# Attention, routed experts and a SwiGLU layer in one kernel: output weights combined on another engine, weight casts issued a block ahead, and activation splits issued earlier

## The chip, the cores and the metric

The kernel runs on one core of a Trainium2 chip. The metric is the device time of one execution in microseconds (us). Before the change three runs took 1058.4, 1061.27 and 1061.85 us, the median being 1061.27 us.

## The reference

Three layers follow one another. The first is attention with a sigmoid in place of the softmax: 4 batches, 12 heads, 448 tokens, heads of 64.

```
scores = (1 / sqrt(64)) * q @ k.T - log(448)
x = sigmoid(scores) @ v                      # 1792 tokens x 768
```

The second is a layer of 8 experts. Each token goes to the expert with the largest logit and is scaled by that expert's softmax probability.

```
e = argmax(x @ w_gate)                        # 768 -> 8
y = prob[e] * (relu(x @ w1[e]) @ w2[e])       # 768 -> 1024 -> 768
```

The third is a dense SwiGLU layer with 1536 hidden columns.

```
g = y @ w2_gate
out = (g * sigmoid(g) * (y @ w2_val)) @ w2_out
```

The weights of the third layer arrive as 64-bit floats. [...]

## The kernel before, in words

**Products in three parts.** TensorE multiplies numbers of a reduced float32 type. To keep the precision each float32 operand is split in a high half (a cast to the reduced type, on ScalarE) and a low half (operand minus high half, on VectorE), and a product is made of three matmuls: high by high, high by low, low by high. `split` (L75) issues the two instructions for one block one after the other.

**Stages.** Attention comes first, then the expert stage (`product` with `kind` 0 and 1, tiles `hps` and `yps`), then the SwiGLU stage (`strassen`, L849, tiles `pa` to `pd`), then the output stage (`product2`, L1406, tiles `oa` to `od`). The third layer's products use the Strassen-Winograd scheme: a 2x2 block product is made of seven products, numbered 1 to 7, of sums and differences of blocks. Their results are added up in PSUM and by VectorE.

**Order of the work.** All of it is written out by hand: each engine executes its instructions in the order in which the program issues them, and an instruction that waits holds up those behind it on its engine. In the expert stage, `when` ties an item of side work to a weight block; in the SwiGLU stage, `at_step` and `later` tie it to a step of the list `steps`. There are 24 rounds of seven products, two rounds to a pair, so 168 steps of nine matmuls each. Most pairs run the products of one round and then those of the other in the order 1, 6, 5, 7, 2, 3, 4. Three pairs (rounds 0 and 1, 10 and 11, 12 and 13) alternate the two rounds and end with 4, 3 instead. `advance` runs after the matmuls of a step are issued: first the evacuations due, then the side work of the step, then the preparation of weights.

**Weight blocks.** `prep` (L730) splits the block for a product five steps ahead of it (`AHEAD`). A block is either a part of a raw tile `w` or a sum `sr`. The sums are made by `sum_w` on GpSimd in the first twelve rounds, stored by SP to DRAM, and loaded again in the other twelve. A raw tile is loaded by SP once its buffer has been released, which the program counts in `left`. In the output stage `prep2` does the same for halves of the activation blocks, and makes their sums on VectorE (`sum_h`).

**Evacuation.** A pair keeps its two rounds side by side in PSUM tiles: `a` for the products 1 and 2, `c` for 5 and 3, `d` for 7 and 4. `c` and `d` are the two buffers of one pool. In `evac` (L884) the products 3 and 4 have `u` added in place in their PSUM tile. `finish_tile` (L869) then takes the value: for the even round, the one of the gate, ScalarE makes a sigmoid `m` and VectorE the product `m` = value times `m`; for the odd round, VectorE makes `h` = value times the even round's `m`, which is stored to DRAM.

**Activation splits.** At the start of the SwiGLU stage `split_all(0, n)` splits the activation block for product `n`: three casts and three subtractions. Block 6 is split ahead of the loop; blocks 5, 7, 4 and 3 at the steps of the products 6, 5, 7 and 4 of round 0.

**Output weights.** They are converted in the background, in six parts `j`: `load_o` loads two raw tiles into a "room", `convert_o` converts them, `combine_o` (L1168) makes four differences of 128x384 on GpSimd, `store_o` (L1176) stores the seven combinations to DRAM by SP. Three parts are done in the expert stage and three in the SwiGLU stage. Near the end of that stage `load_wo` and `split_wo` bring the weights for products 1 and 6; the other 15 pieces follow in the output stage.

Of the kernel before, what the change touches and what calls it, by code (L numbers as in the profile page):

```python
# [9 lines left out]
F32 = mybir.dt.float32  # L10
# [12 lines left out]
def sigmoid_attention_moe_swiglu_kernel(  # L23
# [683 lines left out]
    def a_block(r, i, k):  # L707
        left[r, i - 1] -= 1
        return wraws[r, i - 1][:, (k - 1) * HK:k * HK]
# [20 lines left out]
    def prep(r, n):  # L730
        m = {5: 1, 6: 2, 7: 3, 3: 4}.get(n)
        if m is None:
            s = a_block(r, *{1: (1, 1), 2: (1, 2), 4: (2, 2)}[n])
        else:
            s = sums[r, m]
        hi = early.tile([P, HK], F32R, tag="wgh", name="wgh", bufs=AHEAD + 1)
        lo = early.tile([P, HK], F32R, tag="wgl", name="wgl", bufs=AHEAD + 1)
        split(hi, lo, s)
        wst[r, n] = (hi, lo)
        if m is not None and r < R1:  # L740
            nc.sync.dma_start(wsd[r, m - 1], s)

    state = {"load": 0, "sum": 0, "prep": 0, "now": 0}

# [8 lines left out]
    def sum_to(m):  # L753
        load_more()
        while state["sum"] < min(m, len(steps)) and (steps[state["sum"]][0], 1) in wraws:
            sum_w(*steps[state["sum"]])
            state["sum"] += 1

    def prep_to(m):
        m = min(m, len(steps))  # L760
        while state["prep"] < m:
            sum_to(state["prep"] + 5)
            prep(*steps[state["prep"]])
            state["prep"] += 1
        sum_to(m + 4)

    rows = {}
# [85 lines left out]
    def bank(r, nm):  # L853
        return banks[r // 2, nm][:, r % 2, :TH]
# [29 lines left out]
    def evac(r, n):  # L884
        V = nc.vector
        k = place[r, n] + 1
        if n == 1:
            if (r, "p1") not in sb:
                t = sb[r, "p1"] = et("p", 2)
                nc.scalar.copy(t, bank(r, "a"))  # L890
        elif n == 6:
            t = sb[r, "u"] = et("u", 2)
            V.tensor_add(t, banks.pop((r, "b"))[:, :TH], sb.pop((r, "p1")))
        elif n == 5:
            t = sb[r, "p5"] = et("p", 2)
            nc.scalar.copy(t, bank(r, "c"))  # L896
        elif n == 7:
            t = et("c", 3)
            V.tensor_add(t, bank(r, "d"), sb.pop((r, "p5")))  # L899
            nc.gpsimd.tensor_tensor(t, sb[r, "u"], t, op=ALU.add)  # L900
            finish_tile(k + 2, r, 2, 2, t, nc.gpsimd)
        elif n == 2:
            finish_tile(k, r, 1, 1, bank(r, "a"), V)
        else:
            t = bank(r, {3: "c", 4: "d"}[n])
            V.tensor_add(t, t, sb[r, "u"])
            finish_tile(k + 1, r, *{3: (1, 2), 4: (2, 1)}[n], t, V)

    turn = [2]
# [114 lines left out]
    def when(kind, s, j, f):  # L1024
        at.setdefault((kind, s, j), []).append(f)
# [131 lines left out]
    JO = 3  # L1157
# [7 lines left out]
            room["parts"] = convert(room["ro", x], room["u"], room["w", x].bitcast(F32), True)  # L1165
        room["parts"][g]()

    def combine_o(j):  # L1168
        w0, w1, u = (room[k].bitcast(F32).rearrange("p (x d) -> p x d", x=2)
                     for k in (("w", 0), ("w", 1), "u"))  # L1170
        t4 = room["t4"].bitcast(F32)
        for o, x, y in ((u[:, 0], w0[:, 1], w0[:, 0]), (u[:, 1], w1[:, 1], u[:, 0]),
                        (w0[:, 1], w1[:, 1], w0[:, 1]), (t4, w1[:, 0], u[:, 1])):
            nc.gpsimd.tensor_tensor(o, x, y, op=ALU.subtract)

    def store_o(j):  # L1176
        for n, t in ((2, ("w", 1)), (0, ("w", 0)), (4, "u"), (6, "t4")):
# [70 lines left out]
    with tc.manual_schedule():  # L1248
# [92 lines left out]
        def h_block(q, i, k, h):  # L1341
            j = KD * (k - 1) + K3 * h
            return raw2[q % 2, i][:, j:j + K3].rearrange("p j t -> p (j t)")

        def sum_h(q, m, h):
            V = nc.vector
            if m == 1:
                V.tensor_add(ss[q % 2, 1, h], h_block(q, 2, 1, h), h_block(q, 2, 2, h))
            elif m == 2:
                V.tensor_sub(ss[q % 2, 2, h], ss[q % 2, 1, h], h_block(q, 1, 1, h))  # L1350
            elif m == 3:
                V.tensor_sub(h_block(q, 2, 1, h), h_block(q, 1, 1, h), h_block(q, 2, 1, h))
            else:
                V.tensor_sub(ss[q % 2, 2, h], h_block(q, 1, 2, h), ss[q % 2, 2, h])

        def prep2(q, n, h):
            s = {1: lambda: h_block(q, 1, 1, h), 2: lambda: h_block(q, 1, 2, h),
                 4: lambda: h_block(q, 2, 2, h), 5: lambda: ss[q % 2, 1, h],
                 6: lambda: ss[q % 2, 2, h], 7: lambda: h_block(q, 2, 1, h),
                 3: lambda: ss[q % 2, 2, h]}[n]()  # L1360
            hi = early.tile([P, HK], F32R, tag="wgh", name="hhi", bufs=AHEAD + 1)
            lo = early.tile([P, HK], F32R, tag="wgl", name="hlo", bufs=AHEAD + 1)
            split(hi, lo, s)
            hst[q, n, h] = (hi, lo)
            if h == 0:
                return
            x = 1 if (q, n) == (0, 6) else q if n == 1 and q != 1 else None
            for m in (4,) if n == 7 else (1, 2, 3) if x is not None else ():
                for y in range(2):
                    sum_h(q if n == 7 else x, m, y)  # L1370
            if n == 4 and q + 2 < NQ:
                for i in (1, 2):
                    load_h(q + 2, i)

# [1 line left out]

        def prep2_to(m):
            while state2["prep"] < min(m, len(halves)):
                prep2(*halves[state2["prep"]])
                state2["prep"] += 1  # L1380

        banks2 = {}
        sb2 = {}

# [82 lines left out]
        def at_step(r, n, f, d=0):  # L1467
            todo.setdefault(place[r, n] + d, []).append(f)

        def split_all(p, n, eng=None):  # L1470
            for j in range(K3):
                split_x(p, n, j, eng if j == 2 else None)

        for n in ORD2[2:]:
            if n != 2:
                at_step(0, {5: 6, 7: 5, 4: 7, 3: 4}[n], lambda n=n: split_all(0, n))
        for t in range(2):
            at_step(2 + 2 * t, 1, lambda t=t: load_rows(1, t))
            for j in range(KD):
# [22 lines left out]

        for j in range(JO, KD):
            if j <= JO + 1:
                key = ((1, 6), (R1, 1))[j - JO]
                at_step(*key, lambda j=j: next_room(j))
            b0 = ((2, 1), (R1 + 1, 5), (R1 + 1, 5))[j - JO]
            d = 20 * (j == KD - 1)
            for x in range(2):
                for g in range(4):  # L1510
                    at_step(*b0, lambda j=j, x=x, g=g: convert_o(j, x, g), d + 8 * x + 2 * g)
            at_step(*b0, lambda j=j: combine_o(j), d + 14)
            at_step(*b0, lambda j=j: store_o(j), d + 18)
            if j == JO + 1:
                at_step(*b0, lambda j=j: load_o(j + 1, 0), d + 6)
                at_step(*b0, lambda j=j: load_o(j + 1, 1), d + 14)
# [8 lines left out]
                raw2[0, i] = yt([P, K2, P], "hraw")  # L1525

        early_wo = [(n, i) for n in (1, 6) for i in range(3)]
        base = (NR - 6, ORD[3])
        at_step(*base, first_wo)
        for k, (n, i) in enumerate(early_wo):  # L1530
            at_step(*base, lambda n=n, i=i: load_wo(n, i), 1 + 3 * k)
            at_step(*base, lambda n=n, i=i: split_wo(n, i), 5 + 3 * k)
        for i in (1, 2):
            at_step(*base, lambda i=i: load_h(0, i), 16 + 3 * i)

        def second_raw():
            raw2[1, 1] = raw_tile(post, "z2")
            load_h(1, 1)

        at_step(*base, second_raw, 25)  # L1540

        def first_sums():
            t = hsp.tile([P, FF], F32, tag="hs", name="s2v", bufs=1)
# [107 lines left out]
```

## Time and profile before

| | before |
|---|---|
| runs, us | 1058.4, 1061.27, 1061.85 |
| the profiled execution, us | 1062.1 |
| its span, us | 1060.2 |
| mean granted TensorE clock | 0.991 |
| busy, us: TensorE, its weight loads | 1016.6, 820.2 |
| busy, us: VectorE, ScalarE, GpSimd | 787.4, 590.3, 354.7 |

The span goes from the first to the last instruction of the profiled execution. In the rows below PE is TensorE, PEld its weight loads, DVE VectorE, ACT ScalarE, POOL GpSimd, and SP the engine that issues most transfers; a q behind an engine's name means its sequencer. "L849" is a line of the kernel. Shapes are partitions x elements. Attention takes the first 203 us of the span, the expert stage runs to about 561, the SwiGLU stage to about 893, the output stage to the end.

### The profile page before, as it was taken

What the parts mean: (1) busy time and instruction counts of PE and PEld (TensorE: products, weight loads), DVE (VectorE), ACT (ScalarE), POOL (GpSimd) and SP (SyncE); (2) the same over time, 40 slices, a digit from 0 to 9 for tenths busy, and PEclk for the clock granted to TensorE, in tenths of its full rate; (3) what the DMA queues carried; (4) which work ended last, traced back from release to release, by engine and by line L of the source; (5) the groups of instructions that cost most, each with busy time, mean ns of one, the idle gap of its engine ahead of it and who ended that gap; (6) DMA issues with size and microseconds to landing.
All of it is one profiled execution on the core that took longest, in us unless ns stands there. A gap on an engine that the chain in (4) does not pass through costs nothing. (4 is left out here: it accounts for less than half of the span.)

```text
span 1060.2 us, 16991 instructions
## 1 busy us (share of the span) xinstructions
PE 1016.6 (96%) x5640; PEld 820.2 (77%) x5640; DVE 787.4 (74%) x1279; ACT 590.3 (56%) x941; POOL 354.7 (33%) x303
## 2 busy tenths in 40 slices
PE   8999999999999989999997899999999999999995
PEld 6566556567776767777786789998799899999995
DVE  3776878788877868776687887868988777966651
ACT  6666666446776767676675344455534443733331
POOL 2665566620133331411011665652234222010111
PEclk9999999999999999999999999999999999999998
DMA  8998988756878695688754557534665782653310
GB/s 192 278 269 241 288 245 238 290 179 226 310 249 304 243 345 190 211 324 292 249 180 163 164 160 227 177 120 153 228 220 164 238 247 91 241 167 119 104 46 30
DMA packets 162862, 222.83 MB, mean 210 GB/s; under 512 B 56096, under 2 KB 127008, under 8 KB 162768
## 3 DMA queue, kind: packets, MB, share of 16 engines
q1 hardware_dynamic: 153424, 188.99, 56.3%
q0 software_dynamic: 6864, 31.68, 8.3%
q10 hardware_dynamic: 2480, 1.02, 0.3%
q8 instruction: 46, 0.75, 0.3%
q14 instruction: 48, 0.39, 0.1%
HBM read 217.89 MB, written 55.66 MB: 258 GB/s over the span
## 5 line engine op out<-in xcount | busy, mean ns | idle before, releaser
L985 DVE TENSOR_TENSOR wlo<-wraw,whi 128x768 fp32r<-128x768 f32 (+1 forms) x186 | 204.3, 1123 | 71.0 <-ACT whi L983 66.5
L983 ACT CAST whi<-wraw 128x768 fp32r<-128x768 f32 (+1 forms) x186 | 170.1, 927 | 91.8 <-PE yps L1007 46.9
L242 ACT ACTIVATE a<-sc,logs 112x896 f32<-112x896 f32 x96 | 91.9, 1017 | 60.5 <-PE sc L240 60.4
L849 PE MATMUL pd<-x,wgh 128*128 128x448 f32 x288 | 85.3, 378 | 7.9 <-DVE h L877 4.8
L80 DVE TENSOR_TENSOR wgl<-sr,wgh 128x384 fp32r<-128x384 f32 x96 | 68.9, 722 | 25.9 <-ACT wgh L79 24.9
L849 PE MATMUL pc<-x,wgh 128*128 128x448 f32 x288 | 84.9, 375 | 3.2 <-DVE x L823 1.7
L900 POOL TENSOR_TENSOR c<-u,c 128x448 f32<-128x448 f32 x24 | 35.7, 1489 | 155.1 <-DVE c L899 141.1
L849 PE MATMUL pa<-x,wgh 128*128 128x448 f32 x288 | 82.8, 369 | 0.9 <-PEq L1296 0.9
L251 PE MATMUL pu<-a,vraw 112*64 112x448 f32 x384 | 77.5, 545 | 0.0
L174 POOL TENSOR_SCALAR w<-w 128x768 f32<-128x768 f32 x24 | 54.7, 2278 | 62.1 <-ACT w L162 62.0
L79 ACT CAST wgh<-sr 128x384 fp32r<-128x384 f32 x96 | 48.9, 513 | 35.3 <-PE pd L849 18.2
L849 PEld LDWEIGHTS pd<-x,wgh 128*128 128x128 f32 x288 | 54.5, 193 | 15.5 <-ACT p L896 5.5
L849 PEld LDWEIGHTS pc<-x,wgh 128*128 128x128 f32 x288 | 54.4, 191 | 10.0 <-DVE x L823 2.6
L1007 PE MATMUL yps<-wlo,hh 128*128 128x384 f32 x216 | 56.6, 343 | 3.7 <-DVE wlo L985 3.5
L1007 PE MATMUL yps<-whi,hh 128*128 128x384 f32 x216 | 58.7, 352 | 0.0
L849 PEld LDWEIGHTS pa<-x,wgh 128*128 128x128 f32 x288 | 53.7, 189 | 6.3 <-issue 1.3
L251 PEld LDWEIGHTS pu<-a,vraw 112*64 112x64 f32 x384 | 25.4, 136 | 40.9 <-issue 40.7
L1007 PE MATMUL yps<-whi,hl 128*128 128x384 f32 x216 | 55.5, 337 | 0.1
L80 DVE TENSOR_TENSOR wgl<-w,wgh 128x384 fp32r<-128x384 f32 x72 | 47.5, 661 | 9.4 <-ACT wgh L79 9.3
L849 PE MATMUL pc<-x,wgl 128*128 128x448 f32 x144 | 53.7, 373 | 0.6 <-DVE wgl L80 0.6
L1424 POOL DMA_INDIRECT out_dram<-ot,perm_c x12 | 12.5, 1044 | 124.2 <-DVE hlo L80 71.6
L849 PE MATMUL pd<-x,wgl 128*128 128x448 f32 x144 | 54.0, 375 | 0.0
(310 smaller groups left out, 2572.2 us busy)
## 6 DMA issues: line engine op xcount, KB each, us to landing
wraw<-in_moe_w_dram SPq DMA_DIRECT2D x108, 384.0 KB
wraw<-in_moe_w_dram SPq DMA_DIRECT2D x78, 512.0 KB
ring<-in_moe_w_dram SPq DMA_DIRECT2D x30, 512.0 KB
ring<-in_moe_w_dram SPq DMA_DIRECT2D x40, 384.0 KB
w<-wgd SPq DMA_DIRECT2D x36, 384.0 KB
hraw<-hd SPq DMA_DIRECT2D x13, 768.0 KB
r<-in_moe_w_gate_dram SPq DMA_DIRECT2D x12, 768.0 KB
wgd<-w POOLq DMA_DIRECT2D x24, 384.0 KB, 6.4
```

The source lines that it names most:

```text
L79: nc.scalar.copy(hi, src)
L80: nc.vector.tensor_sub(lo, src, hi.bitcast(F32))
L174: nc.gpsimd.tensor_scalar(w, w, TINY, None, op0=ALU.is_ge)
L242: nc.scalar.activation(am[i][:, c], sc[:CP, :, :S], AF.Sigmoid, bias=logs[:CP], scale=SCALE)
L251: nc.tensor.matmul(pu[h * D:(h + 1) * D, :S], vt[:, h, c], a[:, c, h], start=(c == 0), stop=(c == C - 1))
L849: nc.tensor.matmul(ps, st[:, a], mv[:, j], start=(j == 0 and m == 0 and n not in (2, 3, 4)), stop=(j == K3 - 1 and m == 2), skip_group_che ...
L900: nc.gpsimd.tensor_tensor(t, sb[r, "u"], t, op=ALU.add)
L983: nc.scalar.copy(hi[:, :w], r)
L985: nc.vector.tensor_sub(lo[:, :w0], r[:, :w0], hi[:, :w0].bitcast(F32))
L1007: nc.tensor.matmul(ps[:, m, :w], st[:, a], mv[:, m * w:(m + 1) * w], start=(j == 0 and i == 0), stop=(j == m_ - 1 and i == 2))
L1424: nc.gpsimd.indirect_dma_start(out=out[:, :], out_offset=bass.IndirectOffsetOnAxis(ap=perm_c[:, t:t + 1], axis=0), in_=ot.rearrange("p m d ...
```

## The change

The differences of the output weights move from GpSimd to VectorE, in two halves of two each, which are issued at different places; each half of the stores follows its half of the differences. `prep` issues the cast of a block and returns its subtraction, which is issued behind the next block's cast, with the store of the sum and the release of the raw tile; `prep2` likewise, and its sums are made ahead of a cast instead of behind a split. In `evac` the sum of the products 3 and 4 goes to an SBUF tile instead of staying in PSUM where the pair's last step has the same number. The activation splits of blocks 5, 7, 4 and 3 are issued earlier. The last two rooms and the early output weights get later steps, the latter closer together.

```diff
     def prep(r, n):
...
+            s = wraws[r, i - 1][:, (k - 1) * HK:k * HK]
...
-        split(hi, lo, s)
         wst[r, n] = (hi, lo)
-        if m is not None and r < R1:
-            nc.sync.dma_start(wsd[r, m - 1], s)
+        nc.scalar.copy(hi, s)
+
+        def low():
+            nc.vector.tensor_sub(lo, s, hi.bitcast(F32))
+            if m is None:
+                left[r, i - 1] -= 1
+            elif r < R1:
+                nc.sync.dma_start(wsd[r, m - 1], s)
+        return low
...
-            prep(*steps[state["prep"]])
+            lows.append(prep(*steps[state["prep"]]))
+            if len(lows) > 1:
+                lows.pop(0)()
             state["prep"] += 1
+        if m == len(steps) and lows:
+            lows.pop(0)()
...
-            t = bank(r, {3: "c", 4: "d"}[n])
-            V.tensor_add(t, t, sb[r, "u"])
+            ps = bank(r, {3: "c", 4: "d"}[n])
+            t = et("c", 3) if steps[min(k // 14 * 14 + 13, len(steps) - 1)][1] == n else ps
+            V.tensor_add(t, ps, sb[r, "u"])
...
-    def combine_o(j):
+    def combine_o(h):
...
-        for o, x, y in ((u[:, 0], w0[:, 1], w0[:, 0]), (u[:, 1], w1[:, 1], u[:, 0]),
-                        (w0[:, 1], w1[:, 1], w0[:, 1]), (t4, w1[:, 0], u[:, 1])):
-            nc.gpsimd.tensor_tensor(o, x, y, op=ALU.subtract)
+        for o, x, y in (((u[:, 0], w0[:, 1], w0[:, 0]), (u[:, 1], w1[:, 1], u[:, 0])),
+                        ((w0[:, 1], w1[:, 1], w0[:, 1]), (t4, w1[:, 0], u[:, 1])))[h]:
+            nc.vector.tensor_sub(o, x, y)
...
-        when(*seq[spots[c + 3]], lambda j=j: combine_o(j))
-        when(*seq[spots[c + 4]], lambda j=j: store_o(j))
+        for h in range(2):
+            when(*seq[spots[c + 3 + h] + 1 - h], lambda h=h: combine_o(h))
+            when(*seq[spots[c + 4] + 2 * h], lambda j=j, h=h: store_o(j, h))
...
         def prep2(q, n, h):
+            x = {(0, 6, 1): 1, (q, 1, 0): q}.get((q, n, h))
+            for m in (4,) if (n, h) == (7, 1) else () if x is None or (q, x) == (1, 1) else (1, 2, 3):
+                for y in range(2):
+                    sum_h(q if m == 4 else x, m, y)
...
-            split(hi, lo, s)
             hst[q, n, h] = (hi, lo)
...
+            nc.scalar.copy(hi, s)
+            return lambda: low2(q, n, h, lo, s, hi)
...
-        for n in ORD2[2:]:
-            if n != 2:
-                at_step(0, {5: 6, 7: 5, 4: 7, 3: 4}[n], lambda n=n: split_all(0, n))
+        for n, key in ((7, (1, 2)), (4, (0, 6)), (3, (0, 5))):
+            at_step(*key, lambda n=n: split_all(0, n))
...
-                key = ((1, 6), (R1, 1))[j - JO]
+                key = ((1, 6), (R1 + 1, 5))[j - JO]
...
-            b0 = ((2, 1), (R1 + 1, 5), (R1 + 1, 5))[j - JO]
+            b0 = ((2, 1), (R1 + 2, 6), (R1 + 2, 6))[j - JO]
...
-            at_step(*b0, lambda j=j: combine_o(j), d + 14)
-            at_step(*b0, lambda j=j: store_o(j), d + 18)
+            for h in range(2):
+                at_step(*b0, lambda h=h: combine_o(h), d + 15 + 2 * h)
+                at_step(*b0, lambda j=j, h=h: store_o(j, h), d + 17 + h)
...
-        base = (NR - 6, ORD[3])
+        base = (NR - 4, ORD[0])
...
-            at_step(*base, lambda n=n, i=i: load_wo(n, i), 1 + 3 * k)
-            at_step(*base, lambda n=n, i=i: split_wo(n, i), 5 + 3 * k)
+            at_step(*base, lambda n=n, i=i: load_wo(n, i), 1 + 2 * k)
+            at_step(*base, lambda n=n, i=i: split_wo(n, i), 4 + 2 * k)
...
         split_all(0, 6, None)
+        split_all(0, 5, None)
```

## Rows read from the trace of the kernel before

**Rows 1.** The page, busy us, share of the span, instructions.

```profile
PE 1016.6 (96%) x5640; PEld 820.2 (77%) x5640; DVE 787.4 (74%) x1279; ACT 590.3 (56%) x941; POOL 354.7 (33%) x303
```

**Rows 2.** Waits of TensorE: us in total, times, longest us.

```profile
PE pd L849 <- DVE h L877: 4.8, 2, 2.7
PE yps L1007 <- DVE wlo L985: 3.5, 7, 0.9
...
PE pd L849 <- DVE c L899: 2.6, 4, 1.1
PE hps L1007 <- DVE wlo L985: 1.8, 4, 0.7
PE pc L849 <- DVE x L823: 1.7, 2, 1.2
...
PE pc L849 <- ACT x L822: 0.9, 1, 0.9
```

**Rows 3.** Windows: us, busy of PE, PEld, DVE, ACT, POOL, clock, DMA.

```profile
565.00:600.00 35.00, 28.50 (x124) 23.68 (x122) 27.37 (x43) 17.51 (x39) 17.56 (x15) 0.95 0.46 162
...
750.00:800.00 50.00, 47.47 (x224) 42.68 (x223) 43.51 (x65) 21.02 (x43) 17.93 (x15) 0.97 0.65 212
```

**Rows 4.** The chain of waits: start us, us, what.

```profile
767.53 3.41 PE pd L849 x9
...
774.82 1.85 PE pd L849 x9
...
899.46 3.19 PE ob L1406 x18
...
903.36 3.09 PE ob L1406 x16
```

**Rows 5.** Timeline around the first change of pairs: start us, us, instruction, idle before.

```profile
595.04 0.62 DVE L906 TENSOR_TENSOR pc<-pc,u 128x448 f32<-128x448 f32 x1
...
596.76 0.62 DVE L906 TENSOR_TENSOR pc<-pc,u 128x448 f32<-128x448 f32 x1
...
597.42 0.55 ACT L872 ACTIVATE m<-pc 128x448 f32<-128x448 f32 x1 [3.08 <-DVE pc L906]
...
599.18 0.56 DVE L80 TENSOR_TENSOR wgl<-sr,wgh 128x384 fp32r<-128x384 f32 x1 [1.05 <-ACT wgh L79]
...
600.31 0.62 DVE L877 TENSOR_TENSOR h<-pc,m 128x448 f32<-128x448 f32 x1
```

**Rows 6.** Timeline of ScalarE in the first pair of rounds.

```profile
569.90 0.54 ACT L872 ACTIVATE m<-pa 128x448 f32<-128x448 f32 x1 [2.39 <-PE pb L849]
```

**Rows 7.** Timeline of GpSimd: two of the combines, a gather behind one.

```profile
289.29 6.86 POOL L1174 TENSOR_TENSOR room<-room 128x384 f32<-128x384 f32 x4 [7.35 <-DVE room L178]
...
361.38 7.22 POOL L1174 TENSOR_TENSOR room<-room 128x384 f32<-128x384 f32 x4 [24.93 <-DVE room L178]
...
375.65 1.95 POOL L934 DMA_INDIRECT xg<-xd,perm_g  x1 [0.30 <-PE pt L946]
```

**Rows 8.** One line's instructions: count, ns min/median/max, first and last start.

```profile
L80 DVE TENSOR_TENSOR wgl<-sr,wgh x96: 541/557/1628, 441.9 to 880.9; 128x384 fp32r<-128x384 f32 x96
```

**Rows 9.** Groups on VectorE, 289.3 to 296.1: count, busy us, mean ns, idle.

```profile
L985 DVE TENSOR_TENSOR wlo<-wraw,whi 128x1024 fp32r<-128x1024 f32 x4 | 7.9, 2025 | 0.2 <-ACT whi L983 0.2
```

**Rows 10.** Timelines of TensorE and VectorE in the expert stage.

```profile
291.44 0.74 PE L1007 MATMUL hps<-wlo,xh 128*128 128x512 f32 x2 [0.66 <-DVE wlo L985]
...
368.94 1.21 DVE L985 TENSOR_TENSOR wlo<-wraw,whi 128x1024 fp32r<-128x1024 f32 x1
...
383.89 0.85 PE L946 MATMUL pt<-ident,xg 128*128 128x128 f32 x6 [3.06 <-DMA xg<-xd,perm_g]
```

**Rows 11.** Timeline of VectorE at the start of the output stage.

```profile
901.87 0.96 DVE L80 TENSOR_TENSOR wo<-wo,wo 128x768 fp32r<-128x768 f32 x1 [1.82 <-ACT wo L79]
902.75 1.02 DVE L80 TENSOR_TENSOR hlo<-s2v,hhi 128x384 fp32r<-128x384 f32 x2
```

**Rows 12.** Waits of the engine that issues transfers.

```profile
SPq L703 <- DVE wgl L80: 95.5, 29, 11.4
```

More of the change, by code (lines that the diff above doesn't have):

```diff
@@ L732, in prep @@
         if m is None:
-            s = a_block(r, *{1: (1, 1), 2: (1, 2), 4: (2, 2)}[n])
+            i, k = {1: (1, 1), 2: (1, 2), 4: (2, 2)}[n]
+            s = wraws[r, i - 1][:, (k - 1) * HK:k * HK]
         else:
@@ L737, in prep @@
         lo = early.tile([P, HK], F32R, tag="wgl", name="wgl", bufs=AHEAD + 1)
-        split(hi, lo, s)
         wst[r, n] = (hi, lo)
-        if m is not None and r < R1:
-            nc.sync.dma_start(wsd[r, m - 1], s)
+        nc.scalar.copy(hi, s)
[6 more added lines that the diff above has]
+        return low
+    lows = []
     state = {"load": 0, "sum": 0, "prep": 0, "now": 0}
@@ L1171, in combine_o, with store_o @@
         t4 = room["t4"].bitcast(F32)
-        for o, x, y in ((u[:, 0], w0[:, 1], w0[:, 0]), (u[:, 1], w1[:, 1], u[:, 0]),
-                        (w0[:, 1], w1[:, 1], w0[:, 1]), (t4, w1[:, 0], u[:, 1])):
-            nc.gpsimd.tensor_tensor(o, x, y, op=ALU.subtract)
-    def store_o(j):
-        for n, t in ((2, ("w", 1)), (0, ("w", 0)), (4, "u"), (6, "t4")):
+        for o, x, y in (((u[:, 0], w0[:, 1], w0[:, 0]), (u[:, 1], w1[:, 1], u[:, 0])),
+                        ((w0[:, 1], w1[:, 1], w0[:, 1]), (t4, w1[:, 0], u[:, 1])))[h]:
+            nc.vector.tensor_sub(o, x, y)
+    def store_o(j, h):
+        for n, t in (((2, ("w", 1)), (4, "u")), ((0, ("w", 0)), (6, "t4")))[h]:
             m = 1 if t == "t4" else 2
@@ L1362, in prep2, with low2 @@
             lo = early.tile([P, HK], F32R, tag="wgl", name="hlo", bufs=AHEAD + 1)
-            split(hi, lo, s)
             hst[q, n, h] = (hi, lo)
[L1365 to L1371, printed above, removed]
+            nc.scalar.copy(hi, s)
+            return lambda: low2(q, n, h, lo, s, hi)
+        def low2(q, n, h, lo, s, hi):
+            nc.vector.tensor_sub(lo, s, hi.bitcast(F32))
+            if (n, h) == (4, 1) and q + 2 < NQ:
                 for i in (1, 2):
@@ L1378, in prep2_to @@
             while state2["prep"] < min(m, len(halves)):
-                prep2(*halves[state2["prep"]])
+                lows2.append(prep2(*halves[state2["prep"]]))
                 state2["prep"] += 1
+                while len(lows2) > (state2["prep"] < len(halves)):
+                    lows2.pop(0)()
+        lows2 = []
         banks2 = {}
@@ L1527, in sigmoid_attention_moe_swiglu_kernel @@
         early_wo = [(n, i) for n in (1, 6) for i in range(3)]
-        base = (NR - 6, ORD[3])
+        base = (NR - 4, ORD[0])
         at_step(*base, first_wo)
         for k, (n, i) in enumerate(early_wo):
-            at_step(*base, lambda n=n, i=i: load_wo(n, i), 1 + 3 * k)
-            at_step(*base, lambda n=n, i=i: split_wo(n, i), 5 + 3 * k)
+            at_step(*base, lambda n=n, i=i: load_wo(n, i), 1 + 2 * k)
+            at_step(*base, lambda n=n, i=i: split_wo(n, i), 4 + 2 * k)
         for i in (1, 2):
-            at_step(*base, lambda i=i: load_h(0, i), 16 + 3 * i)
+            at_step(*base, lambda i=i: load_h(0, i), 10 + 2 * i)
         def second_raw():
@@ L1538, in second_raw @@
             load_h(1, 1)
-        at_step(*base, second_raw, 25)
+        at_step(*base, second_raw, 17)
         def first_sums():
```

## The prediction

> **What bounds the kernel now.** The page's busy line comes first: TensorE works 96% of the span and no other engine more than 74% [rows 1], so time can only come out of TensorE's idle time or its clock. The span is 1060.2 us, so 43.6 us of it has no matmul. The waits of TensorE by releaser say which idle time another engine causes [rows 2]: in the SwiGLU stage `pd` waits 4.8 us for the `h` products and 2.6 us for the `c` adds on VectorE, and `pc` waits 1.7 and 0.9 us for the activation splits; together 10.0 us. In the expert (MoE) stage the matmuls wait 3.5 and 1.8 us for the weights' low halves on VectorE, and a row gather holds it up for 3.06 us (its row stands with the combine, below).
>
> The windows add the clock [rows 3]. Three times in the SwiGLU stage, each time after waits that add up to over 2 us, the granted clock falls to half (1.2 GHz); the first and the last of the three stretches show a mean of 0.95 and 0.97. In the chain of waits the nine matmuls behind the last of these waits take 3.41 us, where nine take 1.85 us at 2.4 GHz [rows 4]. Such a wait thus costs its length and 1.56 us behind it; three fallen clocks are 4.7 us. What can be had is about 10.0 + 4.7 in the SwiGLU stage and 4.9 us (3.06 + 1.8), with a little of the 3.5, in the expert stage: some 20 us or 1.9%.
>
> **The wait at a change of pairs.** This is the largest piece. The next pair's `pd` takes the PSUM tile in which the pair before keeps its last product, and that tile is read until the odd round's `h` is made. The timeline shows why `h` is late [rows 5]: the even round's add ends at 595.66 (595.04 + 0.62), yet its sigmoid on ScalarE waits 3.08 us, until the odd round's add into the same tile has ended at 597.38; the cast behind it is late by that; VectorE's subtraction of a weight block, which stands in the queue ahead of the even round's product, waits 1.05 us for that cast; `h` follows only at 600.31, and TensorE is then idle up to 2.7 us [rows 2]. The change touches each link. The even sum goes to a tile of its own, so its sigmoid needs only its own add: 1.72 us earlier (597.38 - 595.66). The subtraction is issued one block behind its cast and no longer waits 1.05 us. That brings `h` forward by 1.7 to 2.8 us, against a wait of 2.7. The two `h` waits are 4.8 us with two fallen clocks at 1.56, 7.9 us; I expect 6.0, nearer the upper end because either link alone covers over half the wait; bounds 0 and 7.9. What is late next is the odd add itself.
>
> **Does the edit do what it says?** Its condition takes the step after the product, `k`, to find the pair. For the odd round's last product `k` is already in the next pair, and where two pairs run their products in different orders (pairs 0 to 1, 4 to 5, 6 to 7) that sum stays in PSUM; 0 to 1 and 6 to 7 are the two places that now wait longest. So only the even sum moves there, and the gain must come from the earlier sigmoid and the unblocked subtraction.
>
> **The first pair of rounds (565 to 592 us).** The sigmoid `m` stands at the head of ScalarE's queue, 2.39 us idle, until 569.90 [rows 6]; the splits of block 5 are behind it, and TensorE waits 1.7 + 0.9 us for them [rows 2], with one fallen clock, 1.56. The change puts block 5's splits ahead of this sigmoid, and those of blocks 7, 4 and 3 two to six steps earlier. No instruction is added: three casts and three subtractions a block. But VectorE is busy 27.4 of 35 us there [rows 3]. With several blocks' splits early, the evacuations move back: I lay VectorE's queue out in its new order, with the durations of now, and find block 5 ready, then the low half of block 7's weights 1.4 us late and the first `c` add 2 us late. By that the first product of `4` moves forward only by 1.9 us. Taken, with a little for the `c` waits behind it: 2.5 us of gain; bounds 0 and 6.8 (1.7 + 0.9 + 2.6 + 1.56). The rest of the short waits gives 0.5.
>
> **The combine on VectorE.** Removed from GpSimd are 24 subtractions of 128x384; four took 6.86 us, 1.72 each [rows 7]. Added to VectorE are 24 of a shape that takes it 0.541 to 1.628 us, median 0.557 [rows 8]: 2.2 us a combine, 13.4 us in all, in pieces of two. What they take away: during the first combine four weight subtractions took 2.025 us each [rows 9], against 1.21 us for the same shape alone [rows 10]. That is 3.3 us lost by VectorE to one combine, more than the 2.2 us added. One of the `hps` waits, 0.66 us, lies inside it [rows 10]; the four of them are 1.8 us [rows 2]. GpSimd's second combine keeps its queue waiting 24.93 us and holds it until 368.6; the row gather behind it is issued at 375.65 [rows 7], and TensorE waits the 3.06 us for a gather until 383.89 [rows 10]. With the combine gone, the stores and the gather can go some 7 us earlier. Bounds in the expert stage: 4.9 us gained (1.8 + 3.06), or 6.7 us lost if each of the six pieces (two times 0.557) stops TensorE in full. I take 3.0 gained: nearest to the rows of the collisions, since a piece is no larger than what a collision costs now. In the SwiGLU stage the other three combines add 6.7 us to VectorE over some 200 us, in its remaining idle time; if that cover failed in full it would be 6.7 us of loss. I count zero, within 1 us.
>
> Rows 9 are one side of a lock. The Trainium skill (SBUF — State Buffer, "SBUF: two separate sides") says that a two-input VectorE instruction and a GpSimd instruction that reads SBUF exclude each other for a whole instruction, and the loser blocks fully. By that rule the added subtractions collide too: GpSimd keeps its sums, and a piece that meets one can cost the 1.628 us of rows 8. Twelve at that price in the SwiGLU stage are 19.5 us of VectorE instead of 6.7. Spread over 200 us they would still lie in its idle time, so the sum would be the same.
>
> **Casts a block ahead.** No instruction is added; the last subtraction of each block goes one step later, with the store of a sum and the release of the buffer that its source lies in. SP's loads of the next blocks wait for such releases now, 29 times [rows 12], and go one product, 1.85 us, later. A block's cast runs five steps, 9 us, ahead of its product, which hides that. Without this cover it would cost up to 1.85 us a round (a rival, below).
>
> **Loads moved later.** Rooms, stores and early output weights go 5 to 11 steps later and closer together; the last of the six early splits comes 13 steps before the stage ends. I count zero; at most 1 us either way.
>
> **Start of the output stage.** Here the change loses. VectorE splits a late output weight, held up until 901.87, and subtracts low halves behind it at 902.75 [rows 11]. Before, the halves up to the sixth lay ahead of that split, and the first product of `6` (899.46, 18 matmuls) ran without a wait [rows 4]. With subtractions one block behind, the second half of this product needs a low half that is queued behind the split: ready at about 903.3 where 901.4 is wanted, 1.9 us in place of the 0.7 us that the next product waits now (902.66 to 903.36 in the chain) [rows 4]. The six sums of the second column group, moved ahead of the cast, lie there too. Loss 1.3 us, bounds 0 and 3.5 (1.9 plus 1.56 of a fallen clock).
>
> **The sum.** Expert stage -3.0, first pair -2.5, changes of pairs -6.0, short waits -0.5, output +1.3: -10.7 us. The profiled execution took 1062.1 us, 1.9 beyond its span and 0.8 above the median of the runs, 1061.27; 1062.1 - 10.7 = 1051.4, or 1050.6 on the median. I say 1051.
>
> **Rivals.** *Half done:* at the two changes of pairs the tile stays held, because the odd sum stays in PSUM and `h` is no earlier; 6.0 us stay away, leaving -4.7: 1056.6. For it is the condition, against it that the delay in rows 5 is in the even sigmoid and the cast. Chance 0.18.
>
> *VectorE is the bound:* stalls move on, since VectorE is 78% busy in the first pair and 87% in 750 to 800 [rows 3]. Of 10.7 us, 7 come back as other waits, leaving -3.7: 1057.6. Against it: part of its idle time is itself a wait for casts, as in rows 5. Chance 0.12.
>
> *Slower, loads late:* the release one step later makes each block's load 1.85 us later. It decides from the point where a load lands after its first reader by more than the five-step lead. With 22 rounds loaded this way and half a step lost in each, 20 us, less the 10.7: 1070.6. Against it, TensorE has no wait on these loads in rows 2. Chance 0.08.
>
> The forecast has 0.56, by itself 1046 to 1055; no gain at all 0.06. Differences under 0.3% (3.2 us) cannot be told from none here. Faster: the forecast and most of the first two rivals, 0.80; within: 0.12; slower: 0.08. The range of 8 in 10 is 1044 (all but 3 of the 20 us) to 1060.
>
> **What would show it.** The even sigmoid without its wait on the odd add; the two `h` waits below 1 us and at most one fallen clock in the SwiGLU stage; the wait on the gather gone; no weight subtraction of 2 us around a combine; a wait of `ob` near 1.9 us at the start of the output stage. The prediction would be wrong if `pd` still waited over 2 us for `h`, if weight waits in the expert stage grew, or if casts waited for block loads.

## The result and the profile after

The changed kernel takes 1048.77 us (median of 4 runs, 1045.71 to 1050.15) where the one before takes 1059.84: ratio 0.9892, 95% interval [0.9859, 0.9925]. In a later set on another chip it took 1049.80 us against 1059.53, ratio 0.991 [0.9883, 0.9938]. It is thus 10 to 11 us faster; 1051.0 had been said. The profiled execution took 1048.04 us (span 1046.3); "again" below is the profiled execution of that later set. The profiled execution before took 1062.1 us, 2.3 more than its median, and the one after 0.7 less than its own: the differences of stages below add up to 13.9 us, some 3 more than the medians lie apart.

The stretches lie between the ends of the last matmuls of a stage, by the starts of the tiles `pu`, `yps` and `hps`, `pa` to `pd`, `oa` to `od`. "First pair" goes from the first `pb` to the next pair's first `pa`. A fallen clock is a stretch at 1.2 GHz, half of the 2.4 GHz elsewhere, behind a wait; the one at the very end, behind the last matmul, is not counted. Most took 3.4 us; one in e_combine and the one in e_old_splits took 6.8 us, and one in e_no_links 10.2 us.

| us | before | after | again | moved by |
|---|---|---|---|---|
| attention | 202.96 | 201.19 | 201.69 | -1.8, -1.3 |
| expert stage | 358.55 | 349.97 | 352.20 | -8.6, -6.4 |
| first pair | 25.81 | 23.29 | 23.38 | -2.5, -2.4 |
| rest of SwiGLU | 305.90 | 301.83 | 299.83 | -4.1, -6.1 |
| output stage | 155.74 | 158.77 | 158.26 | +3.0, +2.5 |
| to the end | 11.28 | 11.28 | 11.29 | 0.0, 0.0 |
| fallen clocks | 3 | 1 | 0 | |

The change touches nothing in attention; its 1.3 to 1.8 us are spread between executions, and two profiles of one program differ by some 2 us in a stage. What follows rests on differences larger than that, or on single waits.

The page's busy line, against [rows 1]:

```profile
PE 1009.2 (96%) x5640; PEld 817.1 (78%) x5640; DVE 794.4 (76%) x1303; ACT 591.6 (57%) x941; POOL 322.9 (31%) x279
```

GpSimd lost 24 instructions and 31.8 us; VectorE, which took them up, is busy 7.0 us more. Waits of TensorE after (us in total, times, longest), against [rows 2]:

```profile
PE pd L862 <- DVE c L912: 3.1, 3, 1.6
PE pd L862 <- DVE h L890: 2.8, 1, 2.8
PE yps L1021 <- DVE wlo L999: 2.5, 5, 0.7
PE ob L1426 <- DVE hlo L1387: 2.0, 1, 2.0
PE pb L862 <- DVE wgl L743: 1.6, 2, 1.0
...
PE hps L1021 <- DVE wlo L999: 1.1, 2, 0.5
...
PE pt L960 <- DMA xg<-xd,perm_g: 0.8, 1, 0.8
...
PE pd L862 <- DVE wgl L743: 0.7, 1, 0.7
```

The wait of 3.06 us for a gather behind the second combine is gone; the 0.8 us left are those of another gather, at the start of the stage (0.26 before). `hps` fell from 1.8 to 1.1, `yps` from 3.5 to 2.5; of two waits for `h` one is left, and the waits of `pc` for the splits are gone. New are `ob` and most of the waits for low halves of weights in the SwiGLU stage. In the expert stage the rows that answer to [rows 9] (groups on VectorE, 289.0 to 296.2) and to [rows 7] (timeline of GpSimd's gathers) are these:

```profile
L999 DVE TENSOR_TENSOR wlo<-wraw,whi 128x1024 fp32r<-128x1024 f32 x5 | 5.9, 1221 | 0.3 <-ACT whi L997 0.2
L1188 DVE TENSOR_TENSOR room<-room 128x384 f32<-128x384 f32 x2 | 1.0, 554 | 0.0
```

```profile
359.10 1.16 POOL L948 DMA_INDIRECT xg<-xd,perm_g  x1 [0.30 <-issue]
368.28 0.99 POOL L948 DMA_INDIRECT xg<-xd,perm_g  x1 [0.30 <-PE hps L1021]
```

A weight subtraction beside a piece of the first combine takes 1.22 us, not 2.03, and a piece 0.55. Collisions have not gone altogether: at the second combine GpSimd's sums of weights now come where its differences were, and a subtraction at 360.2 us takes 2.23 us beside them. In the whole stage 11 of these subtractions took over 1.7 us before and 4 after. No gather stands behind 7 us of GpSimd any more.

At the change from pair 6 to 7 the even sum has its own tile `c`, and `pd` starts with no wait (timeline):

```profile
746.99 0.62 DVE L920 TENSOR_TENSOR c<-pc,u 128x448 f32<-128x448 f32 x1 [0.83 <-PE pc L862]
...
747.65 0.58 ACT L885 ACTIVATE m<-c 128x448 f32<-128x448 f32 x1 [1.33 <-DVE c L920]
...
748.53 0.62 DVE L920 TENSOR_TENSOR pc<-pc,u 128x448 f32<-128x448 f32 x1
...
750.24 0.62 DVE L890 TENSOR_TENSOR h<-pc,m 128x448 f32<-128x448 f32 x1
...
752.30 0.58 PE L862 MATMUL pd<-x,wgh 128*128 128x448 f32 x2
```

The even sigmoid (747.65) now runs ahead of the odd add (748.53), and `h` ends 1.4 us before `pd` starts, where `pd` waited 2.12 us with a fallen clock behind it. The change from pair 0 to 1, which [rows 5] showed, still has a wait:

```profile
582.54 0.58 ACT L885 ACTIVATE m<-c 128x448 f32<-128x448 f32 x1 [0.43 <-DVE c L920]
...
583.77 0.62 DVE L920 TENSOR_TENSOR pc<-pc,u 128x448 f32<-128x448 f32 x1
...
585.67 1.64 DVE L886 TENSOR_TENSOR m<-c,m 128x448 f32<-128x448 f32 x1
585.80 1.02 POOL L717 TENSOR_TENSOR sr<-w 128x384 f32<-128x384 f32 x1
...
587.35 0.62 DVE L890 TENSOR_TENSOR h<-pc,m 128x448 f32<-128x448 f32 x1
588.12 0.65 PE L862 MATMUL pd<-x,wgh 128*128 128x448 f32 x2 [2.85 <-DVE h L890]
```

The sigmoid is early here too, but `m` times `c` takes 1.64 us while GpSimd adds weights, and `h` is late again. In the other profile this wait is 1.68 us and no clock fell behind it; the difference is explained below, with the changes of pairs.

### The profile page after: what moved, and what is told of

It reads as the page before. It is cut to its first block, busy times and chain, and to the rows that moved or that the text cites. A ratio compares the mean times of both kernels' runs of the same rounds, so it can differ in the third digit from the quotient of the medians.

```text
span 1046.3 us, 16920 instructions
## 1 busy us (share of the span) xinstructions
PE 1009.2 (96%) x5640; PEld 817.1 (78%) x5640; DVE 794.4 (76%) x1303; ACT 591.6 (57%) x941; POOL 322.9 (31%) x279
## 5 line engine op out<-in xcount | busy, mean ns | idle before, releaser
L999 DVE TENSOR_TENSOR wlo<-wraw,whi 128x768 fp32r<-128x768 f32 (+1 forms) x186 | 198.8, 1091 | 63.9 <-ACT whi L997 60.3
L743 DVE TENSOR_TENSOR wgl<-sr,wgh 128x384 fp32r<-128x384 f32 x96 | 71.0, 747 | 5.5 <-ACT wgh L740 5.5
L862 PE MATMUL pa<-x,wgl 128*128 128x448 f32 x144 | 52.7, 366 | 0.0
```

The costliest lines, as they stand in the source:

```text
L743: nc.vector.tensor_sub(lo, s, hi.bitcast(F32))
L862: nc.tensor.matmul(ps, st[:, a], mv[:, j], start=(j == 0 and m == 0 and n not in (2, 3, 4)), stop=(j == K3 - 1 and m == 2), skip_group_che ...
L999: nc.vector.tensor_sub(lo[:, :w0], r[:, :w0], hi[:, :w0].bitcast(F32))
```

## The experiments

All medians are device time; each set ran on one chip beside the kernel before (1059.90 us in the first set, 1061.30 in the second, 1059.53 in the third). The last columns are of the profiled execution, in us as above.

| kernel (set) | median | ratio to before, 95% interval | expert | first pair | rest of SwiGLU | output | fallen clocks |
|---|---|---|---|---|---|---|---|
| e_combine (1) | 1053.46 | 0.9927 [0.9899, 0.9955] | 354.30 | 23.31 | 308.25 | 155.65 | 2 |
| e_late_pool (1) | 1055.80 | 0.9961 [0.9945, 0.9977] | 356.04 | 25.70 | 305.73 | 155.61 | 3 |
| e_old_prep2 (1) | 1046.79 | 0.9865 [0.9830, 0.9900] | 352.52 | 23.41 | 302.07 | 156.35 | 1 |
| e_odd_sums (1) | 1049.87 | 0.9902 [0.9865, 0.9938] | 350.59 | 23.39 | 299.73 | 160.65 | 1 |
| e_both (2) | 1046.75 | 0.9853 [0.9826, 0.9881] | 352.91 | 23.32 | 300.75 | 155.81 | 0 |
| e_in_psum (2) | 1050.12 | 0.9891 [0.9864, 0.9918] | 350.01 | 23.23 | 299.78 | 160.50 | 1 |
| e_old_prep (2) | 1054.29 | 0.9932 [0.9911, 0.9952] | 350.21 | 24.77 | 300.80 | 160.75 | 3 |
| e_old_splits (2) | 1051.47 | 0.9896 [0.9868, 0.9923] | 351.52 | 23.77 | 302.74 | 159.20 | 1 |
| e_again (3) | 1049.80 | 0.9910 [0.9883, 0.9938] | 352.20 | 23.38 | 299.83 | 158.26 | 0 |
| e_no_links (3) | 1058.86 | 0.9990 [0.9967, 1.0012] | 352.12 | 27.04 | 303.80 | 160.71 | 4 |
| e_best (3) | 1047.30 | 0.9888 [0.9861, 0.9914] | 349.94 | 23.00 | 300.63 | 155.49 | 0 |

**e_combine: the kernel before with the combine on VectorE alone.** Its halves and their stores lie where the change puts them.

```diff
-        for o, x, y in ((u[:, 0], w0[:, 1], w0[:, 0]), ...
-            nc.gpsimd.tensor_tensor(o, x, y, op=ALU.subtract)
+        for o, x, y in (((u[:, 0], w0[:, 1], w0[:, 0]), ...)[h]:
+            nc.vector.tensor_sub(o, x, y)
```

> The kernel before with one part of the change alone: the differences of the output weights and their stores as after the change, on VectorE in two halves. Theory: the gain in the expert stage is this part's, by freeing GpSimd's queue (gather, scatter) and by taking its subtractions off VectorE's port. Then the stage from the last attention product to the last yps matmul takes 350 to 353 us against 358.5 before (350.0 in the whole change), TensorE's 3.06 us wait for a gather falls below 1 us, no weight subtraction of 128x1024 takes 2 us beside a combine, the SwiGLU and output stages stay within 1.5 us, and the median is 5 to 8 us under before. Rival: most of the 8.6 us is a difference between two executions; then the stage stays above 356 us and the median within 2 us of before.

The median is 6.4 us under before, with an expert stage 4.3 us shorter although one clock fell in it (some 1.6 us, by [rows 4]). Its waits of TensorE:

```profile
PE pd L849 <- DVE h L877: 5.2, 2, 3.1
...
PE yps L1007 <- DVE wlo L985: 2.6, 5, 0.7
...
PE hps L1007 <- DVE wlo L985: 1.1, 2, 0.5
...
PE pt L946 <- DMA xg<-xd,perm_g: 0.9, 1, 0.9
```

The three waits of the expert stage are those of the changed kernel to 0.1 us; both `h` waits are still there. By itself this one part gives most of what the whole change gives.

**e_late_pool: the kernel before, the combine still on GpSimd but two blocks later.** GpSimd's queue is freed for the gather and the collisions with VectorE stay.

```diff
-        when(*seq[spots[c + 3]], lambda j=j: combine_o(j))
+        when(*seq[spots[c + 3] + 2], lambda j=j: combine_o(j))
```

> The kernel before with the combine left whole on GpSimd, but issued two weight blocks later in the expert stage, behind the gather and scatter that stood behind it. It separates the queue from the port. If the queue is what costs, the 3.06 us gather wait goes, weight subtractions beside a combine still take about 2 us, and the expert stage is 3 to 4.5 us shorter than before. If the collisions on the port are what costs, it is less than 1.5 us shorter and the gather wait stays or comes back elsewhere.

GpSimd's timeline, and TensorE's transposes that waited 3.06 us for a gather in [rows 10]:

```profile
364.03 1.44 POOL L934 DMA_INDIRECT xg<-xd,perm_g  x1 [0.30 <-issue]
365.49 6.30 POOL L1174 TENSOR_TENSOR room<-room 128x384 f32<-128x384 f32 x4
```

```profile
378.93 0.82 PE L946 MATMUL pt<-ident,xg 128*128 128x128 f32 x6
```

The gather goes first now and the wait for it is gone. The collisions stay: 13 weight subtractions took over 1.7 us, where before has 11. The median is 4.1 us under before. If the collisions cost as much as before, the queue made about two thirds of what e_combine gave by the medians (4.1 of 6.4 us), or half by the ratios (0.39% of 0.73%); the rest is left for the collisions. In the profile the expert stage is only 2.5 us shorter, less than expected: a gather at its start is waited for 1.5 us, and the waits on `ring` are 3.5 us where they were 2.9.

**e_odd_sums: the changed kernel with the condition looking at the right pair.** The odd sum gets a tile of its own too.

```diff
-            t = et("c", 3) if steps[min(k // 14 * 14 + 13, len(steps) - 1)][1] == n else ps
+            t = et("c", 3) if steps[place[r, n] // 14 * 14 + 13][1] == n else ps
```

> The kernel after with the condition in the evacuation taken from the product's own step instead of the next one, so that the odd round's sum of a pair's last product goes to SBUF too at every change of pairs. Theory: pd waits 2.85 us at the first change of pairs because the odd sum stays in PSUM until h; with this edit that wait falls below 0.6 us, the fallen clock behind it goes, and the SwiGLU stage (last yps matmul to last pd matmul, 325.1 us after) is 3 to 4.5 us shorter; median 1044 to 1046. Rival: the delay lies in VectorE's queue and the port shared with GpSimd; then the wait only moves and the stage gains less than 1 us.

The wait for `h` is gone, but others stand in its place:

```profile
PE pd L862 <- DVE c L912: 4.2, 4, 1.6
...
PE ob L1426 <- DVE hlo L1387: 2.5, 1, 2.5
...
PE pa L862 <- DVE m L886: 1.7, 1, 1.7
```

The rest of the SwiGLU stage (299.73) is that of "again" (299.83), and the median is 1049.87: no gain that can be told from none, where 3 to 4.5 us in the stage had been expected.

**e_in_psum: the changed kernel with the even sum left in PSUM.** Here the even sigmoid waits for the odd add again.

```diff
-            t = et("c", 3) if steps[min(k // 14 * 14 + 13, len(steps) - 1)][1] == n else ps
+            t = ps
```

> The kernel after with the sums of the products 3 and 4 always in PSUM, as before the change. Theory as predicted: the even round's sum in SBUF is one of two links; without it the wait at the change of pairs 6 to 7, gone in after, returns with 1 to 2 us and perhaps a fallen clock, the one at the change 0 to 1 stays near 3 us, and the SwiGLU stage is 1.5 to 4 us longer than after (325.1 us). Rival: the unblocked subtraction alone did it, and the sum in SBUF even costs, since the product made from it met GpSimd on the port (1.64 us against 0.62); then the stage is within 1 us of after or shorter.

The waits did not return. At the change from 0 to 1 (timeline):

```profile
582.79 0.54 ACT L885 ACTIVATE m<-pc 128x448 f32<-128x448 f32 x1 [2.32 <-DVE pc L920]
...
584.05 0.61 DVE L886 TENSOR_TENSOR m<-pc,m 128x448 f32<-128x448 f32 x1
584.18 1.05 POOL L717 TENSOR_TENSOR sr<-w 128x384 f32<-128x384 f32 x1
584.69 0.62 DVE L890 TENSOR_TENSOR h<-pc,m 128x448 f32<-128x448 f32 x1
...
585.47 0.65 PE L862 MATMUL pd<-x,wgh 128*128 128x448 f32 x2 [0.32 <-ACT wgh L740]
```

The sigmoid waits for the odd add again (2.32 us), and yet `h` is early enough: no weight subtraction stands blocked ahead of the product, and the product takes 0.61 us. Part of it at this place is an earlier load (see the changes of pairs below). At 6 to 7 no wait appears either: there the own tile is not needed as long as the casts go a block ahead.

**e_old_prep: the changed kernel with a block's cast and subtraction together again.**

```diff
-            lows.append(prep(*steps[state["prep"]]))
-            if len(lows) > 1:
-                lows.pop(0)()
+            prep(*steps[state["prep"]])
```

> The kernel after with the weight blocks split at once as before (cast and subtraction one behind the other), everything else as after, the output stage too. Theory: the subtraction that waits for its cast holds up VectorE's evacuations; the waits of pd at both changes of pairs return or grow by 0.5 to 1.5 us each, and the SwiGLU stage is 1.5 to 4 us longer than after (325.1 us). Rival: the earlier sigmoid did it alone, and the stage stays within 1 us; or the subtraction a block later even costs at the places where the low half was late (waits of pb, 1.6 us, and pd, 0.7 us, on wgl), and the stage is up to 2 us shorter.

No wait at 6 to 7 here either: the own tile alone suffices too. In the first pair the wait for the `c` adds grows to 3.46 us with a fallen clock behind it (waits of TensorE: total, times, longest), and the median is 1054.29 (0.9932, where the changed kernel has 0.989 to 0.991).

```profile
PE pd L849 <- DVE c L899: 4.9, 3, 3.5
```

**e_no_links: both of these undone.** Even sum in PSUM and cast and subtraction together; combine, early splits and later loads as changed.

> The changed kernel with both links at the changes of pairs undone: the even sum stays in its PSUM tile (the even sigmoid waits for the odd add again) and a weight block's subtraction directly follows its own cast. Theory (either link alone suffices at the change from pair 6 to 7, and the pair of them is the cause): there the wait of pd for h returns, 1.8 to 2.7 us with a fallen clock, and at the change from 0 to 1 it is 2 to 3 us; the SwiGLU stage is 2 to 5 us longer than the changed kernel's 325, at 327 to 330. Rival (the waits went because rooms, stores and early output weights lie elsewhere now, not because of the links): the wait at 6 to 7 stays away as in the changed kernel, SwiGLU stage 324 to 326.5.

The change from 6 to 7 (timeline):

```profile
754.90 0.55 ACT L872 ACTIVATE m<-pc 128x448 f32<-128x448 f32 x1 [2.82 <-DVE pc L907]
...
755.88 0.56 DVE L80 TENSOR_TENSOR wgl<-sr,wgh 128x384 fp32r<-128x384 f32 x1 [1.01 <-ACT wgh L79]
...
757.41 0.62 DVE L877 TENSOR_TENSOR h<-pc,m 128x448 f32<-128x448 f32 x1 [0.44 <-issue]
...
758.18 0.65 PE L849 MATMUL pd<-x,wgh 128*128 128x448 f32 x2 [2.09 <-DVE h L877]
```

This is the chain of [rows 5] again, each link near its length there (3.08 and 1.05), and the clock falls behind the wait. The median is 1058.86, 9.1 us above the changed kernel on the same chip and not to be told from the kernel before. So the links are the cause of the wait at 6 to 7, removing either alone opens this place, and the moved loads are not what did it. The 9.1 us are more than this one place: the first pair is 3.7 us longer (the `c` wait of e_old_prep) and four clocks fell, one in the expert stage, two in the SwiGLU stage (the one in the first pair for 10.2 us) and one in the output stage. At 0 to 1 the wait was 1.47 us, less than the 2 to 3 expected.

**e_old_splits: the changed kernel with the activation splits where they were.**

```diff
-        for n, key in ((7, (1, 2)), (4, (0, 6)), (3, (0, 5))):
-            at_step(*key, lambda n=n: split_all(0, n))
...
-        split_all(0, 5, None)
+        for n in ORD2[2:]:
+            if n != 2:
+                at_step(0, {5: 6, 7: 5, 4: 7, 3: 4}[n], lambda n=n: split_all(0, n))
```

> The kernel after with the activation splits of the first pair of rounds at their old steps. From the first pb matmul to the first pa matmul of the next pair the trace before has 25.8 us, after 23.3 us. Theory: the 2.5 us are the splits' alone; the stretch takes 25.3 to 26.3 us, pc waits over 2 us for x, with a fallen clock. Rival: casts a block ahead already unblocked this pair; then the stretch takes 23.0 to 24.3 us.

The first pair is 0.5 us longer, and the ratio (0.9896) is that of the changed kernel: the early splits give nothing that can be measured. e_combine, which has neither them nor the casts ahead, has the same first pair (23.31) too; no clock fell in it, for a reason that stays open. At 0 to 1 the wait for `h` is 4.18 us here, the longest of all runs, with 6.8 us of fallen clock behind it; why is not shown.

**e_old_prep2, e_both, e_best: the output stage's preparation as before.** Each splits a half at once and makes the sums behind it; e_both adds the odd sums, e_best leaves the even sum in PSUM.

```diff
-            nc.scalar.copy(hi, s)
-            return lambda: low2(q, n, h, lo, s, hi)
+            split(hi, lo, s)
```

> The kernel after with the preparation of the output stage as before: each half block split at once, sums behind the split. Theory: the 3.0 us that the output stage lost (155.9 to 158.9 us of matmuls) come from low halves queued one block behind, first behind the split of a late output weight. Then the stage is back to 155.5 to 156.5 us with one wait of 0.5 to 1 us at its start, and the execution is about 3 us shorter than after (median 1044 to 1047). Rival: the stage is set by when the output weights land; then it stays at 158 to 159 us.

> The kernel after with two edits together: the odd round's sum of a pair's last product goes to SBUF too, and the output stage's preparation is as before (split at once, sums behind it). Each alone left something behind: the first shortened the SwiGLU stage by 2.0 us but its output stage was 1.9 us longer than after (a fallen clock behind a 2.48 us wait of ob), the second shortened the output stage by 2.4 us. Theory: the two add up, because the wait of ob is gone with the old preparation: SwiGLU stage 322.5 to 323.7 us, output stage 156 to 156.8 us, no clock fallen between 20 and 1030 us, median 1043 to 1046 us, 2 to 5 us under after. Rival: SwiGLU's gain is given back at the start of the output stage whatever the preparation, because the late output weights land when they land; then the output stage is 158 us or more and the median within 1.5 us of the version with the old preparation alone (1046.8).

> The changed kernel with its output stage's weight preparation as before (split at once, sums behind the split) and with the sums of the products 3 and 4 in their PSUM tile as before; everything else as changed. Theory (the two terms add up): SwiGLU stage 322.5 to 324, output stage 155.5 to 156.5, no wait of ob over 1 us, at most one fallen clock; median 1043 to 1046, 3 to 6 us under the changed kernel on this chip. Rival (what the PSUM sum gives at the change of pairs is given back at a later wait, as it was in the median when only this was altered): 1046 to 1048, no better than the old weight preparation alone.

The output stage is 155.5 to 156.4 us in all three, 2 to 3 us under the changed kernel's, and the wait of `ob` is absent. The medians are 1046.79, 1046.75 and 1047.30: 2 to 3 us better than the changed kernel. The intervals of the ratios overlap, but e_best ran beside it on one chip (1047.30 and 1049.80), five of its six executions below all six of the changed kernel. What e_both and e_best alter at the changes of pairs adds nothing that can be measured: the sum that both expected (1043 to 1046) did not come, and e_best's rival held. These are the best versions found.

**e_again: the changed kernel as it is**, for the spread.

> The changed kernel itself, unaltered, so that the two others of this chip have it beside them and the spread between profiled executions of one program is seen. All theories: expert stage 349.5 to 352.5 us, first pair about 23.3, SwiGLU stage 324 to 326.5, output stage 158 to 161 with the wait of ob near 2.0 us; median 1047 to 1051.

The median and all stages but the rest of SwiGLU and `ob` (1.4 us instead of 2.0) came as expected.

## Why the prediction came out

1051.0 was said and 1048.77 measured; the direction, the places and most mechanisms were right, and two sizes were off in opposite directions. That the total came within 2.3 us is in part luck: these two errors partly cancel, and the size of the first pair came from another cause than the one given.

- **Expert stage, said -3.0, found -8.6 and -6.4.** This is the mis-sized term. The mechanism was right: no gather behind the combine, and 4 slow weight subtractions in place of 11. But 3.0 took the collisions as the measure and left the freed queue nearly out, which e_late_pool puts at half to two thirds of e_combine's gain. Even the bound of 4.9 was too near: it left out `yps`, which gave 1.0 us more. By the listed waits the difference from before to "again" is 4.3 of its 6.4 us (gather 2.0, `yps` 1.0, `hps` 0.7, `ring` 0.6); `ring` varies by execution (2.9 before, 0.9 after, 2.3 again) and makes much of the difference between the two profiles. The other 2 us lie in no listed wait. TensorE's weight loads waited 3.9 us less for low halves (who waited for them: us, times; before, then after), but how much of that reached the matmuls stays open:

```profile
  PEld yps L1007: 7.5, 12
  PEld hps L1007: 4.7, 7
```

```profile
  PEld yps L1021: 5.5, 9
  PEld hps L1021: 2.8, 5
```

- **First pair, said -2.5, found -2.5, but not for the reason given: luck.** The early splits are worth 0.5; 1.6 is the clock that did not fall, and in e_combine and e_old_splits it did not fall without them. The losses that the reordered VectorE queue was to bring came: `c` late by 1.6 us (said 2; it was 1.06 before), low halves of weights late by 0.6 and 0.7 (said 1.4). Casts a block ahead, priced at nothing, keep this place: without them the `c` wait is 3.46 us. VectorE's idle time on such casts, by the view of the weights' low halves (us, times), shows how much they freed, before and after:

```profile
  ACT wgh L79: 34.1, 36
```

```profile
  ACT wgh L740: 7.9, 9
```

- **Changes of pairs, said -6.0, found -4.1 and -6.1.** Both links are shown at 6 to 7 by e_in_psum, e_old_prep and e_no_links. "Either link alone covers over half the wait" was a slip for the second, 1.05 of 2.65 us; at 6 to 7 either alone nevertheless took all of it. At 0 to 1 the wait stayed (2.85 and 1.68 us), for two reasons. One had been priced at nothing: the even product's operand now lies in SBUF and it meets GpSimd, which costs 1.0 us. The prediction held every VectorE instruction with two inputs to be liable to that; this product was not while its sum lay in PSUM (0.61 us in e_in_psum). The other is a late load. A sum of GpSimd in the first pair waits for a block's load; a cast waits for the sum, and VectorE's subtraction ahead of the two adds for the cast (timelines of VectorE after and of GpSimd again; GpSimd's after is with the rivals):

```profile
578.01 0.82 DVE L743 TENSOR_TENSOR wgl<-sr,wgh 128x384 fp32r<-128x384 f32 x1 [1.77 <-ACT wgh L740]
```

```profile
576.28 1.21 POOL L717 TENSOR_TENSOR sr<-w 128x384 f32<-128x384 f32 x1 [10.12 <-DMA w<-wgd]
```

  The sum starts 3.8 us ahead of the next pair's first `pa` after (575.32 and 579.11) and 5.6 us again (576.28 and 581.93); the odd add, which had been said to be late next, starts 4.7 us behind that `pa` after and 3.0 us again, and `h` ends 8.9 and 7.2 us behind it. e_old_prep2, with this part of the kernel unaltered, has the sum 3.5 us ahead and a wait of 2.85 us. e_best, with the sum 5.6 us ahead and the even sum in PSUM, has `h` end at 6.2 us: the 1.0 us of the product. In e_in_psum the sum was 6.0 us ahead. By this the late load makes the 1.2 us by which the wait of 2.85 us exceeds that of again; it is read from profiles, and no experiment moved the load alone.
- **Output start, said +1.3, found +3.0 and +2.5.** The wait of `ob` is the one foreseen (2.02 us for 1.9). The timeline of VectorE shows it as said, against [rows 11]: the low half stands behind the split of a late weight.

```profile
885.21 0.96 DVE L80 TENSOR_TENSOR wo<-wo,wo 128x768 fp32r<-128x768 f32 x1 [2.44 <-ACT wo L79]
886.09 0.55 DVE L1387 TENSOR_TENSOR hlo<-ss,hhi 128x384 fp32r<-128x384 f32 x1
```

  Missed were two later waits for a low half (0.31 and 0.27 us), behind each of which the stage lies some 0.6 us further back. e_old_prep2, e_both and e_best, with output stages of 155.5 to 156.4, show that nearly all of the loss belongs to the new preparation; its later subtractions and its earlier sums were not told apart.
- **The rivals.** *Half done*: the condition does miss the odd sum, but that costs nothing measurable (e_odd_sums). *VectorE is the bound*: in small; `c` and weight waits of 0.6 to 1.6 us took the place of others, not 7 us. Of the 24 pieces on VectorE one took 1.50 us, the others 0.54 to 0.56. *Loads late*: in small too. In the first pair GpSimd's sums wait for a block's load, and casts for the sums (timeline of GpSimd and ScalarE, after). TensorE is not stopped by it in that pair, but VectorE is late by it at the change from 0 to 1, as told above. Two of the signs that the prediction set against itself thus came, this one and, in one of the two profiles, a wait of `pd` for `h` of over 2 us.

```profile
575.32 1.02 POOL L717 TENSOR_TENSOR sr<-w 128x384 f32<-128x384 f32 x1 [11.98 <-DMA w<-wgd]
...
577.47 0.51 ACT L740 CAST wgh<-sr 128x384 fp32r<-128x384 f32 x1 [9.95 <-POOL sr L717]
```

The parts do not add up: the combine alone gives 6.4 us, undoing the two links costs 9.1, undoing the output preparation gains 2 to 3, and the whole is 10 to 11. Part of this is clocks that fall or don't fall when a wait changes by tenths. How much the later rooms and output weights give by themselves was not tried.

## What to carry to other kernels

An instruction taken off a queue is worth what stood behind it: look for the gather or store that follows a long operation on its engine before pricing the operation itself. Where two links delay one wait, undo them one at a time and together: at the change from pair 6 to 7 either alone changed nothing, and both brought the whole wait back. A reordering that helps one stage (casts a block ahead) can cost in the next, where a late input stands in the same queue; test it stage by stage.

## What the runs showed of the hardware

The same product on VectorE took 0.61 us with its sum in PSUM and 1.64 to 1.67 us with it in SBUF (profiles of e_in_psum; after, again, e_odd_sums), each time beside GpSimd's sums of weights; `h`, with one operand in PSUM, took 0.62 us beside them, and 1.33 us in e_odd_sums with both operands in SBUF. SBUF alone is not what slows it: with both operands in SBUF and no GpSimd sum or product beside it, the product took 0.61 to 0.63 us at every other place (after). The Trainium skill (SBUF — State Buffer, "SBUF: two separate sides") says that a VectorE instruction with two SBUF inputs and a GpSimd instruction that reads SBUF share a port pair as an exclusive lock. These rows agree. Moving a sum out of PSUM to free it can thus make its reader slower.

The clock fell behind waits of 2.09 us (e_no_links), 2.12 (before) and 2.85 us (after), and stayed at 2.4 GHz behind 2.02 us (after) and 2.25 us (`ob` in e_old_splits), so that the length of the one wait did not decide it alone. With a fallen clock behind `ob` the output stage is 160.5 to 160.8 us, without one 158.3 to 159.2.
